# Order of the attention units: the last rows of the first batches as units of their own, behind parts of later batches

## The chip, the cores and the metric

The kernel runs on one core of one Trainium2 chip. Its time is device time in microseconds (us) for one execution: TensorE (PE in the profile), VectorE (DVE), ScalarE (ACT), GpSimd (POOL) and SyncE (SP, which issues DMAs here) work side by side on instruction streams of their own, and the time ends with the last of them. Times of the kernel before are the median of three runs; one further execution was profiled.

## The reference

Two blocks in a row, on 8 batches of 576 rows. The first is attention with 8 heads of 64 columns, in which each row keeps its 32 largest scores; the second is a two-layer MLP on the rows that result.

```python
scores = scale * np.matmul(q, k.transpose(0, 1, 3, 2))      # (8, 8, 576, 576)
kth = np.partition(scores, -32, axis=-1)[..., -32:-31]
attn = softmax(np.where(scores >= kth, scores, -1e9))
x = np.matmul(attn, v).transpose(0, 2, 1, 3).reshape(8, 576, 512)
xn = (x - mean(x)) / np.sqrt(var(x) + 1e-6) * g_ln          # per row
out = x + np.maximum(xn @ w_ch1, 0.0) @ w_ch2               # 512 -> 2048 -> 512
```

q, k and v come as float32; the MLP's gain and weights come as float64, which the kernel reads as pairs of 32-bit words and turns into float32 itself.

## The kernel before, in words

**Units.** A unit is 128 query rows of two heads (a head pair, hp 0 to 3): two tiles of 128 x 576 scores. 576 rows are four such row tiles (qt 0 to 3) and 64 last rows (qt = `J` = 4), which for the two heads share one tile of 128 partitions: a *rest* unit, half as much work for VectorE. There are 8 x 4 x 5 = 160 units. A *job* is one head pair of one batch with a list of row tiles; its units form one group, whose weights are turned into one `pt` tile and multiplied with v together. The list `jobs` (L1027 to L1034) sets the order: for every batch a few *parts* (lists of row tiles), and in each part the four head pairs. Before, batch 0 has the parts [0, 1], [2, 3], [4]; batch 1 has [0, 1], [2, 3, 4]; all later ones [0, 1, 4], [2, 3].

**The step loop** (L1212 to L1361). Step n runs a stage of several units, so that every engine has work: scores of unit n + 2 (TensorE, then ScalarE copies them to `sc`), the selection of unit n on VectorE, the mask of unit n - 1 (ScalarE L496, GpSimd L499) and its exponentials (ScalarE L507), the turning of unit n - 2's weights, and values, output transposes and normalisation of a group that ended two to four units ago. VectorE's selection (`halve`, `select`) first takes the maximum and the minimum of a row's two halves (`hi`, `lo`, L425 and L426), then four rounds of the 8 largest and their replacement (L447, L433); it has two `hi` buffers. GpSimd's `watched` (L466) reads `hi` at the end, so the halving of unit u + 2 waits for the `watched` of unit u.

**Turning.** The weights of a unit must be transposed for the values matmul. Where `u.moved` is set (L1058), VectorE transposes in blocks of 32 (L538) and five DMAs through DRAM do the rest (`move`: one out, four back into `pt`); otherwise TensorE transposes them (L565) and ScalarE copies from PSUM. Before, from the fifth job on, every unit but the last of its group and the rests is moved: 88.

**Heads.** q and k of a head pair are loaded (`load`, L294) and turned by VectorE (`turn_heads`, L326, three transposes) at the pair's first job. The turned k and the later part of q are also written to DRAM (`keep_heads`, pool `turned_kq`, two buffers per head pair, L85), and a later job of the same batch and pair fetches them back (`fetch_heads`). Each job also loads its v (`load_values`) and copies v's last rows into the single tile `ends` (`fill_ends`, GpSimd).

**The MLP.** 256 rows make a block: the row tiles of a part, or the rests of four batches (two head-pair-complete row tiles). A block is *given* (`give`) some steps after the last head pair of its rows is through; then its 64 hidden matmuls (L779) and 56 (the first block: 32 of twice the width, L818) output matmuls (L936) stand in the list `todo`. Eight calls of `fill` in each step take from it as much as `slot(n)` allows: for every later give, the work that will have been given by then, less a reserve of 4 us, is divided by the steps until then, and the least such pace counts. In the first 22 steps it is the difference of the planner's own costs for VectorE and TensorE. After the last unit what is left is worked off without attention between.

**Weights.** 32 pieces of the MLP's weights are loaded, four ahead of the loop and one or two in most of steps 0 to 20 (`batches`). ScalarE and GpSimd split a piece (`split`), VectorE shifts the exponent (`shift`, L176), GpSimd joins it (`join`, L182 and L184). In step n the pieces of `batches[n - 1]` are shifted ahead of the selection (L1236) and joined behind the mask (L1248). When the first block's output is done, GpSimd forms sums of weight blocks (`form_pair`), two of which go to DRAM; later blocks' output matmuls wait for them.

**Start.** L1196 to L1211 load the first two jobs' heads and the first pieces, and compute the scores of units 0 and 1, before the loop; the loads of the second job's q stand on ScalarE's queue.

Of the kernel before, what the change touches and what calls it, by code (L numbers as in the profile page):

```python
# [21 lines left out]
J = 4  # L22
# [7 lines left out]
def compute(  # L30
# [12 lines left out]
    nc = tc.nc  # L43
    P = nc.NUM_PARTITIONS
    B, H, S, D = q.shape
# [5 lines left out]
    NHP = H // 2  # L51
# [5 lines left out]
    def pool(name, bufs, **kw):  # L57
        return ctx.enter_context(tc.tile_pool(name=name, bufs=bufs, **kw))
# [23 lines left out]
    opool = pool("o", 2)  # L82
    xtpool = pool("xt", 1)
    hpool = pool("h", NF // 2)
    turnedpool = pool("turned_kq", 2, space=bass.MemoryType.DRAM)  # L85
    hbmpool = pool("hbm", 4, space=bass.MemoryType.DRAM)
    formpool = pool("forms", 1, space=bass.MemoryType.DRAM)
    psps = pool("ps", 5, space=PSUM)
# [111 lines left out]
    batches = {}  # L200
# [4 lines left out]
    batches = {n: x for n, x in batches.items() if x}  # L205
# [4 lines left out]
    def weights(n, phase):  # L210

        now, coming = batches.get(n, []), batches.get(n + 1, [])
        if phase == 0:
            for x in coming if n < LATE else []:
                x.fetch()
            for x in now[0::2] if n < LATE else []:
                x.split()
        elif phase == 1:  # L220
            for x in now if n >= LATE else now[1::2]:
                x.split()
            for x in coming if n >= LATE else []:
                x.fetch()

    def join_weights(n):
        for x in batches.get(n - 1, []):
            x.join()
# [65 lines left out]
    def load(job, first, second, later=False):  # L294

        job.ins = {}
        for name, src, queue in (("k", k, first), ("q", q, second)):
            t = ldpool.tile([P, S], FP32, tag=name + "in", name=name + "in")

            def part(i, t=t, src=src, queue=queue):  # L300
                head, d0 = 2 * job.hp + i * 32 // D, i * 32 % D
                queue.dma_start(
                    t[i * 32 : (i + 1) * 32, :].rearrange("b (n a) -> b n a", a=32),
                    src[job.b, head, :, d0 : d0 + 32].rearrange("(n b) a -> b n a", b=32),
                )

            for i in range(P // 32):
                if later:
                    age = (4 * len(job.ins) + i) // 2
                    loads.add(lambda i=i, part=part: part(i), -age)  # L310
                else:
                    part(i)
            job.ins[name] = t
# [62 lines left out]
    def scores(u):  # L376

        u.made = [score_half(u, s) for s in range(2)]
        return u.made[0][0][:, HALF:]

    def take_scores(u):
        u.sc = scpool.tile([P, 2, S], FP32, tag="sc", name="sc")
        for t in range(len(u.tiles)):
            for s in range(2):
                nc.scalar.copy(  # L385
                    u.sc[:, t, s * HALF : (s + 1) * HALF], u.made[s][t][:, 0:HALF]
                )
# [25 lines left out]
    def halve(u):  # L413

        nt = len(u.tiles)  # L420
        u.lo = lopool.tile([P, 2, HALF], FP32, tag="lo", name="lo")
        u.hi = hipool.tile([P, 2, HALF + 8 * low_rounds], FP32, tag="hi", name="hi")
        a, b = u.sc[:, 0:nt, 0:HALF], u.sc[:, 0:nt, HALF:S]
        lo, hi = u.lo[:, 0:nt], u.hi[:, 0:nt, 0:HALF]
        nc.vector.tensor_tensor(hi, a, b, ALU.max)  # L425
        nc.vector.tensor_tensor(lo, a, b, ALU.min)  # L426
# [66 lines left out]
    def mask(u, t):  # L493
        if u.e is None:
            u.e = epool.tile([P, 2, S], FP32, tag="e", name="e")
        nc.scalar.activation(  # L496
            u.e[:, t], u.sc[:, t], AF.Relu, bias=u.edge[:, t : t + 1], scale=-STEEP
        )
        nc.gpsimd.tensor_tensor(u.e[:, t], u.e[:, t], u.sc[:, t], ALU.subtract)  # L499
# [56 lines left out]
    def turn(u):  # L556

        g = u.group
        i0 = place_of(u)
        q0 = i0 * 32  # L560

        def part(t):
            ps = turned()
            for c in range(J):
                nc.tensor.transpose(  # L565
                    ps[:, c * P : (c + 1) * P], u.e[:, t, c * P + t * R : (c + 1) * P + t * R],
                    ident[:],
                )
            if u.rest:
                both = ps[:].rearrange("p (c h n) -> p h c n", h=2, n=R)  # L570
                for h in range(2):
                    nc.scalar.copy(
                        g.blocks[:, h, i0 : i0 + R // 32],
                        both[:, h].rearrange("p c (i n) -> p i c n", n=32),
                    )
            else:
                nc.scalar.copy(
                    g.blocks[:, t, i0 : i0 + P // 32],
                    ps[:].rearrange("p (c i n) -> p i c n", c=J, n=32),
                )  # L580

        def last():
            turn_ends(u)()

        heads = () if u.moved else range(len(u.tiles))
        return [lambda t=t: part(t) for t in heads] + [last]
# [58 lines left out]
    def take_values(g):  # L645
        g.oT = otpool.tile([P, GQ], FP32, tag="oT", name="oT")
        nc.scalar.copy(g.oT[:, 0 : g.nq], g.av[:, 0 : g.nq])
# [376 lines left out]

    jobs = []  # L1027
    for b in range(B):
        parts = [[0, 1], [2, 3], [J]]
        if b:  # L1030
            parts = [[0, 1], [2, 3]]
            parts[b < 2].append(J)
        for qts in parts:
            jobs += [Job(b, hp, [qts]) for hp in range(NHP)]  # L1034
    units = []
    for j in jobs:
        j.groups = [Group(j, qts) for qts in j.groups]
# [8 lines left out]
    fresh = []  # L1046
# [8 lines left out]
    CONVERTING = max(n for n in batches if batches[n]) + 2  # L1055
    EARLY = jobs[NHP].first

    for u in units[EARLY:]:  # L1058
        u.moved = not u.rest and u is not u.group.units[-1]


    for j, after_j in zip(jobs, jobs[1:] + [None]):
# [14 lines left out]
    for j in jobs:  # L1077
        if j.hp == NHP - 1:
            b = j.b
# [26 lines left out]
    def at(i):  # L1106
        return units[i] if 0 <= i < N else None
# [92 lines left out]
        x.fetch()  # L1200
    turn_heads(fresh[0])
    nc.sync.dma_start(grow[:], g_ln.rearrange("(c p) -> c p", p=P))
    load(fresh[1], nc.sync, nc.scalar)
    scores(units[0])
    take_scores(units[0])
    halve(units[0])
    scores(units[1])
    take_scores(units[1])
# [3 lines left out]
    for n in range(END):  # L1212
# [8 lines left out]
        u, nxt, mk = at(n), at(n + 1), at(n - 1)  # L1221
# [3 lines left out]
        parts = turn(ex) if ex and not ex.moved else []  # L1225
# [7 lines left out]
        if quick:  # L1233
            values(g)
            take_values(g)
        for x in batches.get(n - 1, []):  # L1236
            x.shift()
        spare = None
        for x in ahead:
# [4 lines left out]
        if mk:  # L1244
            prepare(mk)
            for t in range(len(mk.tiles)):
                mask(mk, t)
        join_weights(n)  # L1248
        if mk and doubt is not None:
            watch(mk)  # L1250
        if plain_done[0] is not None and plain_done[0] < n - 1:
# [85 lines left out]
        if last_rest and last_rest.rest and last_rest.job.b % 2:  # L1337
            hp = last_rest.job.hp
# [9 lines left out]
            select(u, 3)  # L1348
        if nxt:
            halve(nxt)  # L1350
        weights(n, 1)
        if g and not quick and g.job.hp == NHP - 1:
            for qt in g.qts:
# [18 lines left out]
@with_exitstack  # L1372
def kernel(
    ctx: ExitStack,
    tc: tile.TileContext,
    *operands: bass.AP,
):
    nc = tc.nc
    doubt = ctx.enter_context(tc.tile_pool(name="doubt", bufs=1)).tile(
        [1, 1], I32, tag="doubt", name="doubt"  # L1380
    )
    compute(tc, *operands, low_rounds=1, doubt=doubt[:])
    again = nc.values_load(  # L1383
        doubt[:], min_val=0, max_val=1,
        skip_runtime_bounds_check_because="a comparison's result",
    )
    with tc.If(again > 0):
        compute(tc, *operands, low_rounds=2, doubt=None)
# [31 lines left out]
```

## Time and profile before

| | us |
|---|---|
| median of 3 runs | 1628.69 (1627.76 to 1628.86) |
| the profiled execution | 1625.28 |
| its span, first to last instruction | 1623.1 |
| busy: PE / DVE / ACT / POOL | 1486.5 / 1370.2 / 1058.0 / 1030.9 |
| mean granted TensorE clock | 0.965 of full |

The profile page gives for each engine its busy time, its share of the span and its instructions; then the span in 40 slices with one digit each for the busy share in tenths, and the clock granted to TensorE in tenths (PEclk). A table by stretch has one row for each piece of time: its ends and length, the busy time of PE, PEld (TensorE's weight loads), DVE, ACT and POOL with the number of instructions, the granted clock, the DMA engines' mean share and the GB/s they moved. A line of the waits has the waiting instruction, "<-" what released it, and the total, the number and the longest of these waits in us. A line in order of time has start, length, engine, source line and operation, and in brackets the idle time before it. Ends of matmuls are modelled, and the span is some 2 us shorter than the execution's own time.

### The profile page before, as it was taken

What the parts mean: (1) busy time and instruction counts of PE and PEld (TensorE: products, weight loads), DVE (VectorE), ACT (ScalarE), POOL (GpSimd) and SP (SyncE); (2) the same over time, 40 slices, a digit from 0 to 9 for tenths busy, and PEclk for the clock granted to TensorE, in tenths of its full rate; (3) what the DMA queues carried; (4) which work ended last, traced back from release to release, by engine and by line L of the source; (5) the groups of instructions that cost most, each with busy time, mean ns of one, the idle gap of its engine ahead of it and who ended that gap; (6) DMA issues with size and microseconds to landing.
All of it is one profiled execution on the core that took longest, in us unless ns stands there. A gap on an engine that the chain in (4) does not pass through costs nothing. (4 is left out here: it accounts for less than half of the span.)

```text
span 1623.1 us, 27069 instructions
## 1 busy us (share of the span) xinstructions
PE 1486.5 (92%) x7770; PEld 1124.5 (69%) x7770; DVE 1370.2 (84%) x3971; ACT 1058.0 (65%) x2984; POOL 1030.9 (64%) x1489
## 2 busy tenths in 40 slices
PE   3579678689979899999999999999999999999997
PEld 2346346467757677777777777777777777778886
DVE  5997978989999999999999999999999989882000
ACT  5878765566757686777666767677677766763221
POOL 6878976855546565667566747576657574746244
PEclk9779989799989999999999999999999999999999
DMA  6625644444646456445564556546554554522211
GB/s 159 167 69 160 195 119 130 153 138 118 197 121 202 126 144 172 158 152 133 162 192 131 142 148 176 161 122 174 144 174 149 146 148 156 157 90 85 71 34 54
DMA packets 367206, 228.27 MB, mean 141 GB/s; under 512 B 248772, under 2 KB 337352, under 8 KB 367048
## 3 DMA queue, kind: packets, MB, share of 16 engines
q1 hardware_dynamic: 362312, 225.86, 48.5%
q8 instruction: 64, 1.05, 0.3%
q10 hardware_dynamic: 4736, 0.59, 0.2%
q14 instruction: 94, 0.77, 0.2%
HBM read 154.01 MB, written 72.35 MB: 139 GB/s over the span
## 5 line engine op out<-in xcount | busy, mean ns | idle before, releaser
L499 POOL TENSOR_TENSOR e<-e,sc 128x576 f32<-128x576 f32 x288 | 405.1, 1425 | 421.7 <-ACT e L496 323.9
L779 PE MATMUL hps<-xT,w 128*128 128x256 f32 x2304 | 542.1, 385 | 6.0 <-ACT xT L741 3.8
L779 PEld LDWEIGHTS hps<-xT,w 128*128 128x128 f32 x2304 | 430.3, 193 | 76.2 <-issue 10.8
L447 DVE MAX8 m<-hi 128x8 f32<-128x296 f32 (+1 forms) x1152 | 469.8, 442 | 0.1
L433 DVE MATCH_REPLACE8 hi<-m,hi 128x288 f32<-128x288 f32 (+1 forms) x864 | 377.1, 441 | 0.0
L936 PE MATMUL ops<-w,h 128*128 128x256 f32 x1360 | 322.4, 384 | 3.4 <-DMA w<-forms 3.4
L936 PEld LDWEIGHTS ops<-w,h 128*128 128x128 f32 x1360 | 254.0, 193 | 41.7 <-issue 5.0
L496 ACT ACTIVATE e<-sc,m 128x576 f32<-128x576 f32 x288 | 209.3, 769 | 90.1 <-PE scps L599 89.0
L507 ACT ACTIVATE e<-e,m 128x576 f32<-128x576 f32 x288 | 226.8, 790 | 32.3 <-POOL e L499 31.3
L385 ACT COPY sc<-scps 128x288 f32<-128x288 f32 x576 | 187.0, 402 | 63.3 <-POOL e L499 49.8
L425 DVE TENSOR_TENSOR hi<-sc 128x576 f32<-128x576 f32 (+1 forms) x160 | 134.3, 840 | 68.4 <-POOL watched L466 64.0
L802 ACT ACTIVATE h<-hps 128x512 f32<-128x512 f32 x144 | 87.3, 607 | 121.3 <-PE hps L779 120.7
L632 PE MATMUL av<-pt,vb 128*64 128x256 f32 (+2 forms) x1088 | 143.2, 405 | 0.8 <-ACT pt L604 0.6
L426 DVE TENSOR_TENSOR lo<-sc 128x576 f32<-128x576 f32 (+1 forms) x160 | 135.4, 846 | 0.0
L538 DVE STREAM_TRANSPOSE sc<-e 128x512 f32<-128x512 f32 x176 | 113.9, 682 | 22.3 <-ACT e L507 22.3
L404 PE MATMUL scps<-kT,late_qT 64*128 64x288 f32 (+3 forms) x832 | 123.4, 415 | 7.8 <-ACT sc L385 5.7
L936 PE MATMUL ops<-wt,s 128*128 128x256 f32 x544 | 128.7, 381 | 0.4 <-POOL s L866 0.4
L439 DVE MAX8 hi<-lo 128x8 f32<-128x288 f32 x288 | 117.5, 443 | 0.0
L404 PE MATMUL scps<-kT,qT 64*128 64x288 f32 x512 | 91.7, 470 | 24.8 <-DVE qT L331 23.5
L565 PE MATMUL tp<-ident,e 128*128 128x128 f32 x448 | 73.3, 291 | 44.6 <-ACT e L507 29.7
L936 PEld LDWEIGHTS ops<-wt,s 128*128 128x128 f32 x544 | 100.1, 190 | 16.0 <-issue 2.3
L404 PEld LDWEIGHTS scps<-kT,late_qT 64*128 64x128 f32 (+1 forms) x832 | 70.6, 169 | 58.0 <-issue 18.0
(107 smaller groups left out, 1846.5 us busy)
## 6 DMA issues: line engine op xcount, KB each, us to landing
turned<-sc SPq DMA_DIRECT2D x88, 512.0 KB, 2.9
pt<-turned SPq DMA_DIRECT2D x352, 128.0 KB, 2.8
w<-forms SPq DMA_DIRECT2D x136, 256.0 KB, 4.1
vb<-in_v_dram SPq DMA_DIRECT2D x68, 288.0 KB, 3.6
raw<-in_moe_w_ch_dram SPq DMA_DIRECT2D x32, 512.0 KB, 5.3
kT<-kept SPq DMA_DIRECT2D x36, 288.0 KB, 3.3
kin<-in_k_dram SPq DMA_DIRECT2D x128, 72.0 KB, 2.6
kept<-kT SPq DMA_DIRECT2D x32, 288.0 KB, 3.0
```

The lines of the kernel that those rows point to most:

```text
L385: nc.scalar.copy(u.sc[:, t, s * HALF : (s + 1) * HALF], u.made[s][t][:, 0:HALF])
L404: nc.tensor.matmul(ps[i * R : i * R + ql, o : o + width], qT[r, q0 : q0 + ql], kT[r, k0 : k0 + width], start=True, stop=True,)
L425: nc.vector.tensor_tensor(hi, a, b, ALU.max)
L426: nc.vector.tensor_tensor(lo, a, b, ALU.min)
L433: nc.vector.match_replace(x, m[:, t, :], x, LOWEST)
L447: nc.vector.max(m[:, t, :], u.hi[:, t, 0:width])
L496: nc.scalar.activation(u.e[:, t], u.sc[:, t], AF.Relu, bias=u.edge[:, t : t + 1], scale=-STEEP)
L499: nc.gpsimd.tensor_tensor(u.e[:, t], u.e[:, t], u.sc[:, t], ALU.subtract)
L507: nc.scalar.activation(u.e[:, t], u.e[:, t], AF.Exp, bias=u.bias[:, t : t + 1], scale=-scale, accum_out=g.den[:, col : col + 1],)
L632: nc.tensor.matmul(av[h * D : (h + 1) * D, 0 : g.nq], vb[:, h * (J + 1) + c, :], g.blocks[:, h, 0 : g.nq // 32, c, :], start=(c == 0), sto ...
L779: nc.tensor.matmul(ps[0][:, side * N : (side + 1) * N], w1[:, c, f * P : (f + 1) * P], self.xT[:, c, 0:N], start=(c == 0), stop=(c == NC - 1),
L936: nc.tensor.matmul(bank[name][:, 0:Q], a(j), rhs, start=first and j == 0, stop=(j == G - 1), skip_group_check=not first,)
```

## The change

`jobs` is no longer built by a loop over batches. A list `order` of (batch, row tiles) is written out: batch 0's rows 0 to 3, then batch 1's, then half of batch 2, and only then the rests of batch 0 as four jobs of one unit each; the rests of batches 1, 2 and 3 follow in the same way behind parts of later batches. Batches 4 and 5 have their rests with rows 2 and 3. Batches 6 and 7 have them with rows 0 and 1, and their rows 2 and 3 come last of all. That makes 80 jobs in place of 68, and lone rests in steps 40 to 43, 60 to 63, 72 to 75 and 84 to 87, where before the only four stood in steps 16 to 19. As the heads of up to three batches are now needed again later, `turned_kq` gets five buffers.

`moved` is set job by job: a unit is moved unless it is a rest or the last of its job; in batches from 2 on the last unit of head pairs 0 and 2 is moved too, unless a rest follows. 92 units are moved.

At the start the loads of the second job stand behind the first unit's scores and their copies. The four pieces of `batches[-1]` are shifted at the end of step 0, behind the halving of unit 1, and joined after that; from step 1 on both stand where they stood.

```diff
-    turnedpool = pool("turned_kq", 2, space=bass.MemoryType.DRAM)
+    turnedpool = pool("turned_kq", 5, space=bass.MemoryType.DRAM)
...
-    jobs = []
-    for b in range(B):
-        parts = [[0, 1], [2, 3], [J]]
-        if b:
-            parts = [[0, 1], [2, 3]]
-            parts[b < 2].append(J)
-        for qts in parts:
-            jobs += [Job(b, hp, [qts]) for hp in range(NHP)]
+    rows, rest = ([0, 1], [2, 3]), [J]
+    order = [(0, rows[0]), (0, rows[1]), (1, rows[0]), (1, rows[1])]
+    order += [(2, rows[0]), (0, rest), (2, rows[1]), (3, rows[0]), (1, rest)]
+    order += [(3, rows[1]), (2, rest), (4, rows[0]), (3, rest), (4, rows[1] + rest)]
+    order += [(5, rows[0]), (5, rows[1] + rest)]
+    order += [(6, rows[0] + rest), (7, rows[0] + rest), (6, rows[1]), (7, rows[1])]
+    assert B == 8
+    jobs = [Job(b, hp, [qts]) for b, qts in order for hp in range(NHP)]
...
-    for u in units[EARLY:]:
-        u.moved = not u.rest and u is not u.group.units[-1]
+    for j, nj in zip(jobs, jobs[1:] + [None]):
+        for u in units[max(j.first, EARLY) : j.last + 1]:
+            u.moved = not u.rest and (
+                u.i < j.last or (j.b > 1 and j.hp % 2 == 0) and nj is not None and not units[nj.first].rest
+            )
...
-    load(fresh[1], nc.sync, nc.scalar)
     scores(units[0])
     take_scores(units[0])
+    load(fresh[1], nc.sync, nc.scalar)
     halve(units[0])
...
-        for x in batches.get(n - 1, []):
+        for x in batches.get(n - 1, []) if n else []:
             x.shift()
...
-        join_weights(n)
+        if n:
+            join_weights(n)
...
         if nxt:
             halve(nxt)
+        if n == 0:
+            for x in batches[-1]:
+                x.shift()
+            join_weights(0)
         weights(n, 1)
```

## The prediction

> **What bounds the kernel now.** I read the page's busy shares and slices first, then the same numbers by stretches of the planner's steps, then the waits of VectorE (DVE), then single steps in order of time. Step n begins where VectorE starts the n-th `hi<-sc` maximum (L425, counted from 0); everything below is cut there.
>
> The page, busy shares and slices of 40.6 us:
>
> ```profile
> PE 1486.5 (92%) x7770; PEld 1124.5 (69%) x7770; DVE 1370.2 (84%) x3971; ACT 1058.0 (65%) x2984; POOL 1030.9 (64%) x1489
> ...
> PE   3579678689979899999999999999999999999997
> ...
> DVE  5997978989999999999999999999999989882000
> ...
> PEclk9779989799989999999999999999999999999999
> ```
>
> TensorE (PE) has holes in the first fourteen slices, VectorE stops three slices before the end, and TensorE alone runs on. The same by stretch; the cuts are the starts of steps 20, 32, 88 and 149:
>
> ```profile
> core 0: us, PE busy (x) PEld busy (x) DVE busy (x) ACT busy (x) POOL busy (x), PEclk, DMA share, GB/s
> 0.00:227.50 227.50, 149.30 (x699) 93.19 (x699) 187.57 (x513) 171.90 (x436) 179.95 (x193) 0.89 0.55 151
> 227.50:352.00 124.50, 101.68 (x513) 73.22 (x513) 109.00 (x300) 70.84 (x205) 85.09 (x112) 0.88 0.44 128
> 352.00:825.20 473.20, 449.95 (x2404) 339.07 (x2403) 462.71 (x1371) 331.55 (x975) 289.11 (x439) 0.97 0.54 154
> 825.20:1365.40 540.20, 538.89 (x2918) 415.62 (x2917) 511.30 (x1494) 377.61 (x1091) 348.60 (x529) 1.00 0.53 153
> 1365.40:1623.10 257.70, 246.64 (x1242) 203.44 (x1240) 99.59 (x295) 106.07 (x281) 128.20 (x220) 0.99 0.28 87
> ```
>
> Call them A to E. In C VectorE works 462.71 of 473.20 us: it sets the pace. In D it idles 28.9 us and TensorE is full; in E TensorE alone counts. What ends VectorE's idle time in steps 10 to 31 (113.7 to 352 us):
>
> ```profile
> DVE hi L425 <- POOL watched L466: 17.8, 10, 3.9
> DVE wt L176 <- POOL wt L164: 14.6, 9, 3.5
> ```
>
> There GpSimd (POOL), busy with the weight conversion, is the last to release VectorE. So three regimes: GpSimd with VectorE in A and B, VectorE in C, TensorE in D and E. Steps 50, 51 and 52 in order of time show VectorE's price of a unit:
>
> ```profile
> 501.57 0.73 DVE L425 TENSOR_TENSOR hi<-sc 128x576 f32<-128x576 f32 x1
> 509.12 0.70 DVE L425 TENSOR_TENSOR hi<-sc 128x288 f32<-128x288 f32 x1
> 513.43 1.30 DVE L538 STREAM_TRANSPOSE sc<-e 128x512 f32<-128x512 f32 x2
> 514.99 0.74 DVE L425 TENSOR_TENSOR hi<-sc 128x576 f32<-128x576 f32 x1
> ```
>
> A bare whole unit takes 7.55 us (501.57 to 509.12). A last-row unit ("rest") takes some 4.2: step 51 is 5.87, with a move of 1.37 (1.30 busy and its start-up) and a little waiting.
>
> **What the skill says.** The Trainium skill, "Perfetto Trace Analysis", Identifying the Most-Contended Engine, warns that matmul busy time is no measure of how full TensorE is. The trace agrees: C shows it 95% busy while the steps have VectorE's length, so I add up matmuls instead. "TensorE: Matmul & The Clock Gate", Part 1, says that the array falls to half its clock after about 3.4 us idle; here the granted clock is 0.89, 0.88 and 0.97 in A, B and C against 1.00 in D, so holes there cost twice. "SBUF — State Buffer", Who interferes with whom, says that a VectorE instruction with two SBUF inputs contends with a GpSimd instruction that reads SBUF: the halving pair of step 1 took 1.37 and 1.82 us under GpSimd's joins, and 0.76 and 0.75 in step 0 without them.
>
> **The change, part by part.** One MLP matmul is two records; 78 records in 17.00 us at 1454.78 (L779) make 0.436 us each. The order of both programs gives the MLP matmuls per stretch, before and after: B 117 and 130, C 641 and 690, D 823 and 745, E 465 and 481. A has 90 in both. The planner spreads what has been given until the next batch rows arrive. With rows 0 to 3 of batches 0 and 1 coming without rests between them, rows arrive at steps 9, 20, 28, 36 and not at 9, 19, 32, 44, and the pace is some 12.5 a step from step 22 to 148, steps 26 to 28 apart, where the formed weights are awaited (before: 9 to 10, then 12, then 14). About 78 matmuls, 34 us, leave D, where they are on the path, for B and C, where TensorE had holes. That is the gain; the rest is cost.
>
> *A.* Steps 0 to 15 process the same units. Without the four shifts behind the first halving VectorE loses waits of 2.67, 3.12 and 1.20 us in step 0, and with ScalarE's four load issues (2.99 us at 7.12) behind the first score copies it starts about 2 us sooner. But the four joins on GpSimd (11.2 us, 22.07 to 33.3) now start only after the second halving, and step 2's halving waits for GpSimd's `watched` behind them; before, that row ended 0.1 to 2.1 us ahead of the halving in steps 2 to 9. So of the 9 us I take 1; the bounds are +2 and -7. Steps 16 to 19 hold whole units where four rests stood. Those rests took 41.5 us; whole units under conversion took 10.90, 12.44 and 10.64 (steps 13 to 15), 45.2 for four: +3.7. Two more head turns (1.41 us each) half hidden: +1.6. A: 227.5 - 1 + 3.7 + 1.6 = 232.
>
> *B.* Twelve whole units and no rest. Steps 20 and 21 like before, 22. Steps 23 to 26 are GpSimd's: subtract 2.8, form pair 5.2 to 6.4, 1.6 hidden banks of 1.36, small ones 0.5, or 11.2 each, 45. The other six at some 10 (before: 9.3 to 11.5, and 13.8 after a burst of 11.8 us of MLP that is now 9.2): 61. B: 128, against 124.5.
>
> *C.* Forty whole units and sixteen rests (before 43 and 13). VectorE in the whole ones: 40 x 7.55 = 302, 27 moves x 1.37 = 37, 8 head turns x 1.4 = 11, 2 pairs of row statistics x 1.6 = 3, 353; VectorE-bound steps ran 1 to 2% over such sums (steps 52 to 59: 69.6 for 68.8), so 359. The rests now stand in four runs of four. A run costs VectorE 20 us but TensorE 35: 50 MLP matmuls 21.8, and scores (1.2 a unit), transposes (0.6 a bank), values (2.65 for 256 columns, 1.12 for 64) and output transposes (0.38) less their overlap, 13.5. How far may TensorE fall behind? Its lateness reaches VectorE through ScalarE's in-order queue, the subtraction and `watched`: when TensorE is ahead, `watched` ends 4.2 us after the selection (steps 37 to 44), in D 6 to 9, and then the halving waits. So a run absorbs 3 to 5 us, which the whole units behind it give back. A run: 32; four: 128. C: 487, against 473.2.
>
> *D.* Forty-five whole units, sixteen rests, interleaved as before: 340 + 66, 41 moves 56, 12 head turns 17, 6 pairs of statistics 10, 489 of VectorE, and TensorE with 745 x 0.436 = 325 and 150 of attention at 475, no longer over it. Before, 823 x 0.436 + 160 = 519 ran in 540. In steps 56 to 76, TensorE at 0.94 of VectorE, the time was 178.7 for a VectorE sum of 173, 1.033. I take 1.04: 507, against 540.2, or -33.
>
> *E.* 16 more MLP matmuls and two row turns, +7.9; steps 149 to 155 have matmuls enough where they had not, -2.5. E: 263.
>
> The twelve more lone rests bring twelve more head fetches (two DMAs each) and twelve value loads, and four more moves bring five DMAs each, on SyncE's queue. At some 0.75 MB a rest beside a DMA share of 0.53 I cost them nothing; the step of margin between fetch and scores hides them, and without it each would cost its 3.3 us landing time. The larger DRAM pool costs nothing.
>
> Sum of the span: 232 + 128 + 487 + 507 + 263 = 1617, against 1623.1: about -6. The rows are of an execution of 1625.28 us; the three runs' median is 1628.69. I put the median at 1622.
>
> **The rivals.** *Runs of rests stall (slower).* Each lone rest refills the one `ends` tile: TensorE's values, GpSimd's refill, TensorE's next values. The only lone rests of before took 41.5 us, with a wait of 3.42 us on `ends` at 228.42. For it: the same buffers. Against: there the refill stood behind weight joins. If a run costs 37 and not 32, +20: 1642. It decides from a run of 34.5 on. *VectorE and GpSimd keep D slow.* D's idle ends on `watched`, which also follows GpSimd's own queue; at 1.07 of VectorE's sum D takes 522 and the whole 1637, slower too. *Only re-dealt.* A and B come 6 us dearer than I say, since nothing there is TensorE's: 1628, the same. *More absorbed.* Runs at 28 and D at 497: 1622 - 16 - 10 = 1596; TensorE's waits of the first slices speak for it.
>
> **How the numbers follow.** Forecast (1605 to 1625) 0.45; more absorbed 0.12; only re-dealt 0.14; stalling runs 0.20; slow D 0.09. 0.2% of 1628.69 is 3.3 us, about what a measurement of this kernel can tell from no change. Faster 0.57, same 0.14, slower 0.29. The range leaves a tenth on each side: 1603 to 1643. The forecast's own is 1605 to 1625.
>
> **What would show it.** Step 88 of the new program should start near 847 us, later than before's 825.2; step 149 near 1354, earlier than 1365.4; VectorE's idle time between them under 20 us, not 28.9; and each run of four 128x288 halvings should span 30 to 34 us. TensorE's holes in slices 6 to 14 should shrink. I am wrong if the runs span over 35 us, if D does not come under 515, or if step 32 starts past 368.

## The result, and the profile after

| us | before | after |
|---|---|---|
| median | 1627.76 (8 runs, 1626.18 to 1628.95) | 1618.16 (8 runs, 1612.28 to 1624.14) |
| ratio after to before | | 0.9941 (95%: 0.9922 to 0.996) |
| the profiled execution / its span | 1625.28 / 1623.1 | 1617.02 / 1615.1 |

The kernel is faster by 0.6%, some 10 us. After's runs lie further apart (0.7%) than before's (0.2%), so differences between profiles of a few microseconds are read with care below.

First the page of the kernel after, its busy shares and its slices (40.4 us each):

```profile
PE 1487.4 (92%) x7954; PEld 1131.2 (70%) x7954; DVE 1371.2 (85%) x3979; ACT 1057.7 (65%) x2988; POOL 1033.9 (64%) x1513
...
PE   3578769799999999999999999999999999999997
...
DVE  5997998899989997999978999999999999666100
```

The busy times of TensorE's matmuls and of the other three engines moved by 3 us at most (TensorE's weight loads grew by 7), so nothing was saved in work. What changed is where TensorE's holes are: before, slices 6 to 14 read `786899798`, now `697999999`. The holes that C had (from slice 9 on) are filled. VectorE works on a little longer at the end (the 666 before the last 100).

The table by stretch of the kernel after, cut as before at the starts of steps 20, 32, 88 and 149 (ends, length, busy PE, PEld, DVE, ACT, POOL with counts, clock, DMA share, GB/s):

```profile
0.00:233.30 233.30, 152.79 (x656) 95.83 (x657) 201.51 (x562) 176.26 (x442) 186.39 (x196) 0.86 0.55 150
233.30:356.70 123.40, 107.84 (x525) 77.67 (x526) 114.10 (x323) 77.27 (x217) 89.21 (x113) 0.87 0.47 133
356.70:837.00 480.30, 472.61 (x2784) 367.09 (x2783) 448.79 (x1319) 339.86 (x993) 302.66 (x477) 1.00 0.61 171
837.00:1349.50 512.50, 505.60 (x2748) 384.85 (x2746) 498.45 (x1472) 357.36 (x1058) 320.32 (x505) 1.00 0.57 162
1349.50:1615.10 265.60, 248.58 (x1247) 205.73 (x1246) 108.34 (x309) 106.98 (x279) 135.28 (x223) 0.99 0.30 94
```

| | A | B | C | D | E | span |
|---|---|---|---|---|---|---|
| before | 227.5 | 124.5 | 473.2 | 540.2 | 257.7 | 1623.1 |
| forecast | 232 | 128 | 487 | 507 | 263 | 1617 |
| after | 233.3 | 123.4 | 480.3 | 512.5 | 265.6 | 1615.1 |
| after less before | +5.8 | -1.1 | +7.1 | -27.7 | +7.9 | -8.0 |

One stretch gains and three pay for it. D lost 27.7 us. MLP matmuls counted in the two traces between VectorE's marks are 822.5 in D before and 756.5 after, 66 or 28.8 us fewer; 49 of these are now in C, 10 in E and 6.5 in B. (In the order of the program 78 leave D. TensorE runs behind VectorE's marks, so some of what belongs to C is worked off in D.) In D after, TensorE is still busy in 505.6 of 512.5 us, and VectorE now in 498.5. VectorE's idle time in D is 14.0 us (before 28.9). What ends VectorE's waits in steps 10 to 31 (113.7 to 356.7 us) after:

```profile
DVE hi L425 <- POOL watched L466: 13.3, 8, 3.9
DVE wt L176 <- POOL wt L164: 7.3, 5, 2.0
```

Both are GpSimd's and both are smaller than before (17.8 and 14.6). Inside C, the four runs of lone rests (28.8, 30.5, 30.0 and 29.6 us) and the whole units between them, from the table by stretch:

```profile
356.70:429.60 72.90, 72.22 (x403) 55.38 (x402) 72.83 (x221) 53.29 (x153) 48.53 (x74) 1.00 0.70 196
429.60:458.40 28.80, 28.80 (x185) 22.37 (x184) 20.86 (x61) 20.75 (x63) 9.97 (x16) 1.00 0.57 173
458.40:605.20 146.80, 141.96 (x799) 109.17 (x798) 146.33 (x430) 101.47 (x291) 98.46 (x156) 0.99 0.60 167
605.20:635.70 30.50, 29.50 (x189) 23.14 (x188) 21.96 (x61) 21.65 (x65) 10.85 (x16) 1.00 0.56 167
635.70:705.60 69.90, 69.90 (x421) 55.28 (x419) 69.03 (x211) 51.17 (x152) 51.12 (x81) 1.00 0.49 145
705.60:735.60 30.00, 29.34 (x187) 22.48 (x186) 25.10 (x68) 20.50 (x62) 18.26 (x29) 1.00 0.64 174
735.60:807.40 71.80, 71.29 (x427) 56.51 (x426) 71.02 (x213) 51.63 (x148) 47.08 (x75) 1.00 0.68 183
807.40:837.00 29.60, 29.60 (x189) 22.77 (x189) 21.66 (x61) 19.39 (x61) 18.39 (x33) 1.00 0.57 168
```

The DVE column carries the whole units: 72.83 of 72.90, 146.33 of 146.80, 69.03 of 69.90, 71.02 of 71.80. The PE column carries the runs: TensorE is busy 117.2 of their 118.9 us, VectorE 89.6. But TensorE is nearly full in the whole units too, so this table does not say by itself which engine sets them. Two experiments do.

### The profile page after: what moved, and what is told of

Same layout as the page of the kernel before. It is cut to its first block, busy times and chain, and to the rows that moved or that the text cites. A ratio compares the mean times of both kernels' runs of the same rounds, so it can differ in the third digit from the quotient of the medians.

```text
span 1615.1 us, 27577 instructions
## 1 busy us (share of the span) xinstructions
PE 1487.4 (92%) x7954; PEld 1131.2 (70%) x7954; DVE 1371.2 (85%) x3979; ACT 1057.7 (65%) x2988; POOL 1033.9 (64%) x1513
## 4 chain that ended last, share of the span: by engine, by line
PE 51%; DVE 25%; POOL 10%; DMA 5%; ACT 5%; issue 2%; SPq 1%; ACTq 0%; DVEq 0%; POOLq 0%
PE hps L779 20%; PE ops L936 15%; DVE m L447 7%; DVE hi L433 6%; PE scps L404 6%; PE av L632 5%; POOL e L499 4%; DVE sc L538 3%; DVE lo L426 2%; DVE hi L425 2%; DVE hi L439 2%; DMA pt<-turned 2%; DMA turned<-sc 2%; PE av L639 2%; PE tp L565 2%
## 5 line engine op out<-in xcount | busy, mean ns | idle before, releaser
L496 ACT ACTIVATE e<-sc,m 128x576 f32<-128x576 f32 x288 | 209.3, 769 | 70.4 <-PE scps L599 69.6
L632 PE MATMUL av<-pt,vb 128*64 128x256 f32 (+2 forms) x1280 | 148.9, 375 | 5.5 <-DMA kept<-kT 2.4
L538 DVE STREAM_TRANSPOSE sc<-e 128x512 f32<-128x512 f32 x184 | 119.2, 684 | 12.5 <-ACT e L507 7.1
L632 PEld LDWEIGHTS av<-pt,vb 128*64 128x64 f32 x1280 | 81.2, 141 | 56.0 <-issue 7.1
## 6 DMA issues: line engine op xcount, KB each, us to landing
pt<-turned SPq DMA_DIRECT2D x368, 128.0 KB, 2.8
```

The source lines that it names most:

```text
L496: nc.scalar.activation(u.e[:, t], u.sc[:, t], AF.Relu, bias=u.edge[:, t : t + 1], scale=-STEEP)
L538: nc.vector.transpose(blocks.rearrange("p (j t c n) -> p j t c n", j=ni, t=2, c=J)[:, :, t], u.e[:, t, t * R : t * R + JP].rearrange("p (c ...
L632: nc.tensor.matmul(av[h * D : (h + 1) * D, 0 : g.nq], vb[:, h * (J + 1) + c, :], g.blocks[:, h, 0 : g.nq // 32, c, :], start=(c == 0), sto ...
```

## The experiments

"Whole" and "runs" below are the two kinds of row of the last table, summed: in the kernel after, whole 361.4 and runs 118.9 us. Ratios are to the kernel before, run beside each.

### Which engine sets the whole units and the runs: tensor_plus and vector_plus

Both add work to steps 32 to 87 (C) of the changed kernel alone, without changing its values.

```diff
 tensor_plus
+                if c == 0 and side == 0 and 31 < now[0] < 88:
+                    nc.tensor.matmul(
+                        ps[0][:, 0:N], w1[:, c, f * P : (f + 1) * P], self.xT[:, c, 0:N],
+                        start=True, stop=True,
+                    )
                 nc.tensor.matmul(
 vector_plus
         nc.vector.tensor_tensor(lo, a, b, ALU.min)
+        if 32 < u.i < 89 and nt == 2 and u.i % 4 != 3:
+            nc.vector.tensor_tensor(lo, a, b, ALU.min)
```

> The changed kernel with 47 hidden matmuls of the MLP done twice in steps 32 to 87 (stretch C), 47 x 0.436 = 20.5 us of TensorE; the second writes the same values over the first. Theory: since the change TensorE sets C's length (busy 472.6 of 480.3 us), so C grows by 15 to 21 us and the kernel takes 1631 to 1640. Rival, the prediction's own view that VectorE sets C and TensorE's work fills holes: C grows by under 8 us, 1618 to 1625.

> The changed kernel with the minimum of the halving done twice for 30 whole units of steps 33 to 87 (stretch C), 30 x 0.75 = 22.5 us of VectorE; the second writes the same values. Theory: TensorE sets C, and VectorE's 31 us of idle time there take most of it: C grows by 0 to 9 us, 1618 to 1627. Rival, the prediction's view that VectorE sets C: it grows by 15 to 23 us, 1632 to 1641.

Measured: tensor_plus 1630.12 us (ratio 1.0021, 1.0008 to 1.0034), vector_plus 1649.19 us (1.014, 1.0122 to 1.0158): 12 and 31 us above the changed kernel. The theory that I held by then gave 15 to 21 us to the TensorE work in C and 0 to 9 to the VectorE work; C grew by 14.1 and 35.4. The rival, the prediction's view, gave under 8 and 15 to 23, so neither held as it was put. The first four rows of C, tensor_plus:

```profile
356.90:430.90 74.00, 74.00 (x408) 57.34 (x408) 73.93 (x222) 52.91 (x153) 48.48 (x74) 1.00 0.69 190
430.90:462.10 31.20, 30.75 (x198) 23.96 (x195) 21.06 (x62) 20.74 (x63) 10.05 (x16) 1.00 0.56 166
462.10:609.80 147.70, 145.11 (x822) 112.84 (x823) 145.97 (x431) 102.16 (x293) 99.22 (x156) 1.00 0.59 165
609.80:641.40 31.60, 31.36 (x201) 24.69 (x198) 21.97 (x62) 21.69 (x65) 10.94 (x16) 1.00 0.55 164
```

and the first two runs of whole units of vector_plus:

```profile
352.50:431.10 78.60, 74.11 (x411) 56.80 (x410) 78.36 (x226) 53.90 (x154) 48.39 (x74) 1.00 0.66 183
...
459.60:622.50 162.90, 147.06 (x810) 112.37 (x809) 162.42 (x442) 101.15 (x291) 102.21 (x156) 0.97 0.54 150
```

Lengths in C, whole and runs, of all kernels that keep the changed order of C:

| | whole | runs | C |
|---|---|---|---|
| after | 361.4 | 118.9 | 480.3 |
| tensor_plus | 366.4 (+5.0) | 128.0 (+9.1) | 494.4 |
| vector_plus | 396.8 (+35.4) | 118.9 (0.0) | 515.7 |
| order_76 | 349.0 (-12.4) | 130.7 (+11.8) | 479.7 |
| weighted | 357.4 (-4.0) | 106.9 (-12.0) | 464.3 |
| pace_held | 364.2 (+2.8) | 123.6 (+4.7) | 487.8 |

VectorE's extra work (its busy time in C rose from 448.79 to 484.45, by 35.7) comes out whole, 35.4 us, in the whole units. The edit left the rests alone, so it says nothing of VectorE's worth in the runs. TensorE's 20.5 us come out at 14.1. In the order of the program 17 of the 47 added matmuls (7.4 us) stand in the steps of the runs and 30 (13.1 us) in those of the whole units; the runs grew by 9.1 us and the whole units by 5.0, so TensorE carries part of its work from the whole units into the runs behind them. In the whole units VectorE is idle for only 2.2 of 361.4 us. So VectorE sets the whole units, with TensorE close behind it, and TensorE sets the runs, as the prediction had it. What fell is my theory that TensorE had become the limit of all of C, read off a PE column that was 98% full, and with it the rival's view that TensorE's work would mostly fill holes.

### The rule of what is moved: order_76, and the same in the old order, before_76

```diff
 order_76 (on the changed kernel)
-    for j, nj in zip(jobs, jobs[1:] + [None]):
-        for u in units[max(j.first, EARLY) : j.last + 1]:
-            u.moved = not u.rest and (
-                u.i < j.last or (j.b > 1 and j.hp % 2 == 0) and nj is not None and not units[nj.first].rest
-            )
+    for u in units[EARLY:]:
+        u.moved = not u.rest and u is not u.group.units[-1]
 before_76 (on the kernel before)
         u.moved = not u.rest and u is not u.group.units[-1]
+        if u.job.b in (1, 2, 3) and len(u.group.units) == 3 and u.i == u.job.first + 1:
+            u.moved = False
```

> The changed kernel with the old rule for moved units: every unit but the last of its job and the rests, which makes 76 and not 92. Sixteen moves fewer take 16 x 1.37 = 22 us from VectorE (ten of them between steps 32 and 87, two up to step 148, four after) and give TensorE some 16 x 1.2 = 19 us and ScalarE as much. My theory, VectorE sets the pace to step 87 and TensorE after step 149: 10 x 1.37 less a little in the first, +5 in the last, 1610 to 1620, near the changed kernel's 1618. Rival, the turned units are where the gain comes from: TensorE's 19 us come back, 1630 to 1637.

> The kernel before with 12 fewer units moved, 76 in all: in the groups of three of batches 1 to 3 only the first unit is moved, which lies in steps 20 to 80. Theory: a move costs VectorE 1.37 us and TensorE's turning fills holes that C has anyway, so C gets 8 to 14 us shorter, in the old order too: 1613 to 1620, and half or more of what order_76 has over the kernel before is not from the order. Rival: TensorE and ScalarE pay as much for the turning as VectorE saves: 1624 to 1632.

Measured: order_76 1610.24 us (0.9899, 0.988 to 0.9919), 8 us faster than the change as it was made; before_76 1623.69 us (0.9984, 0.9975 to 0.9993), a gain of 3. C and D of order_76, and the wait of its VectorE in C:

```profile
356.40:836.10 479.70, 479.03 (x2866) 373.08 (x2865) 437.83 (x1299) 351.79 (x1014) 307.64 (x477) 1.00 0.54 150
836.10:1344.60 508.50, 505.69 (x2770) 385.62 (x2768) 494.79 (x1466) 361.01 (x1064) 321.57 (x505) 1.00 0.55 157
```

```profile
DVE hi L425 <- POOL watched L466: 33.4, 16, 4.1
```

In C, ten fewer moves take 11 us off VectorE. The whole units get 12.4 us shorter, and the runs 11.8 us longer: TensorE, which now turns those units itself, arrives later at the runs (22 more MLP matmuls, 9.6 us, fall between their marks, though the program has as many of them in those steps), and VectorE waits for `watched` 33.4 us instead of 23.1. Nothing is left of it. In D, three fewer moves and 3.7 us less of VectorE come out at 4.0 us. The profiles differ by 5.4 us of span, D being most of it; the rest of the 8 is within the spread of runs. The time lies in the range of the theory, but not on its grounds: C was to get shorter by about ten moves, E longer by 5 us, and neither did. before_76 shows the same balance in the old order: VectorE's busy time in C fell by 9.9 us (462.71 to 452.84), its wait on `watched` there rose from 8.2 to 17.3, and C went from 473.2 to 472.0, where the theory asked for 8 to 14 us. So the 16 extra moves cost 8 us where the whole change gained 10, and the order, at 76 moves and with the new start, which the next experiment finds to be worth nothing, is worth 1623.69 - 1610.24 = 13 us (the two were run in different sets, whose kernels before had medians 0.2 us apart).

### The start alone: start_alone

The kernel before with the edits of the start and nothing else.

```diff
-    load(fresh[1], nc.sync, nc.scalar)
     scores(units[0])
     take_scores(units[0])
+    load(fresh[1], nc.sync, nc.scalar)
...
-        for x in batches.get(n - 1, []):
+        for x in batches.get(n - 1, []) if n else []:
...
-        join_weights(n)
+        if n:
+            join_weights(n)
...
+        if n == 0:
+            for x in batches[-1]:
+                x.shift()
+            join_weights(0)
```

> The kernel before, with only the start of the change: loads of the second job behind the first score copies, the first four shifts and joins at the end of step 0. My theory: step 0 loses its waits of 7 us and the first halving comes 1 to 2 us sooner, but GpSimd's four joins start later by as much, and the halving of step 2 waits for GpSimd; by step 10 no more than 1 us is left. 1626 to 1628.5, ratio 0.999 to 1.0005. Rival, the early gain is kept because VectorE sets the pace afterwards: 1619 to 1621, ratio 0.995, and the order of units would then be worth nothing.

Measured: 1625.92 us, ratio 0.9994 (0.9983 to 1.0004): no difference. Where the time goes is seen in VectorE's waits from 0 to step 10 of this kernel:

```profile
DVE hi L425 <- POOL watched L466: 9.1, 2, 8.7
```

Before, the same line stood at 0.4 us. In the changed kernel step 1 begins at 19.5 us instead of 29.1, but step 2 at 40.1 instead of 42.0 and step 10 at 113.1 instead of 113.7, with the same wait (8.4, the longest 8.1).

### Where the MLP stands: pace_held and weighted

pace_held keeps the early rows from being spent early; weighted halves the pace in the sixteen steps of lone rests and raises it elsewhere.

```diff
 pace_held
+        if 31 < n < 56:
+            even = min(even, 4.4)
         return max(0.0, even) / SLOTS
 weighted
+    def room(n):
+        u = at(n)
+        return 0.5 if u and u.rest and len(u.group.units) == 1 else 1.0
...
-                    even = min(even, (left - RESERVE) / (m - n))
+                    even = min(even, (left - RESERVE) * room(n) / sum(map(room, range(n, m))))
```

> The changed kernel with the MLP's pace held at 4.4 us a step in steps 32 to 55, as it was in the kernel before; 39 MLP matmuls (17 us) go from steps 32 to 87 into steps 88 to 148 (651 and 784 of them in place of 690 and 745). My theory, the gain is work taken out of the late stretch: steps 44 to 59 keep their time because VectorE sets it, the run of rests at step 40 gets 4 us shorter, and steps 88 to 148 get 8 to 14 us longer, 1622 to 1628. Rival, the pace does not matter and the order itself gains by other waits: 1612 to 1616.

> The changed kernel with the planner's pace halved in the sixteen steps of a lone rest, 26 MLP matmuls in a run of four in place of 49; the others go mostly to steps 88 to 148 (799 in place of 745). My theory, a run is as long as TensorE's work in it: a run falls from about 30 us to 21 to 24, four of them 24 to 36 us in all, and steps 88 to 148 get 12 to 20 us longer because TensorE's sum (499) passes VectorE's (489) there: 1598 to 1612. Rival, a run is held by the one tile of v's last rows, which TensorE and GpSimd hand to each other: runs stay at 29 to 30 us and the late steps get longer, 1630 to 1638.

Measured: pace_held 1637.46 us (1.006, 1.004 to 1.008); weighted 1615.54 us (0.9939, 0.9915 to 0.9962). C and D of pace_held:

```profile
361.00:848.80 487.80, 466.17 (x2707) 358.06 (x2706) 447.77 (x1320) 338.81 (x989) 292.39 (x458) 0.98 0.60 167
848.80:1374.40 525.60, 521.08 (x2814) 399.57 (x2815) 503.48 (x1472) 363.22 (x1063) 336.02 (x524) 1.00 0.56 160
```

and of weighted:

```profile
354.90:819.20 464.30, 451.73 (x2692) 349.57 (x2691) 449.18 (x1319) 336.23 (x988) 293.55 (x459) 1.00 0.63 176
819.20:1343.10 523.90, 521.95 (x2827) 401.08 (x2827) 501.46 (x1471) 361.50 (x1063) 334.25 (x524) 1.00 0.56 160
```

pace_held returns half of the MLP matmuls that the order had taken from D (784 in D in place of 745, 39 x 0.436 = 17.0 us), and D grows by 13.1, as expected (8 to 14). The kernel lost 19 us in the median and not the 4 to 10 expected. Its profiled execution, 1643.72 us, is the longest of its five and 26.8 us of span over the changed kernel's. Of these A and B have 4.3, where the edit changes nothing, C 7.5, though it has 39 fewer MLP matmuls, and E 1.9. In C the third and fourth row of whole units, which now take more MLP work, are 3.4 and 2.9 us longer, with TensorE busy in 73.3 of 73.3 and 74.2 of 74.7 us. And the first run of rests, which was to be 4 us shorter, is 3.3 longer (32.1 us). With 38 MLP matmuls there instead of 48, TensorE comes to the values of a unit before the transfers in front of them have landed:

```profile
442.97 3.68 PE L632 MATMUL av<-pt,vb 128*64 128x256 f32 x16 [5.09 <-DMA late_qT<-kept]
454.74 1.95 PE L632 MATMUL av<-pt,vb 128*64 128x256 f32 x16
```

It stands still for 5.1 us. The record of the granted clock shows half of full speed from 441.5 to 448.3 us, beginning 3.6 us after TensorE fell idle, and the same 16 matmuls take 3.68 us there and 1.95 in the next group: this hole cost twice, as the prediction says of holes. VectorE then waits 7.8 us for `watched`; the longest such wait in the changed kernel's C is 3.7. So the MLP matmuls in this run also cover transfers, which neither the prediction nor this experiment's expectation had counted. Of the 20.6 us that C and D lose here, D's 13.1 are what half of its relief is worth; the rest has these other causes.

weighted gave its runs 26 or 27 MLP matmuls instead of 48 to 50, in the order of the program. They shrank by 12 us to 26.7 each, not to the 21 to 24 that I expected for VectorE's 20. With the prediction's own terms TensorE needs 26 x 0.436 + 13.5 = 24.8 in a run, and it is busy 24.8; VectorE is busy 23.2. What holds the remaining 2 us was not tested. C got 16.0 us shorter, D 11.4 longer, and the medians differ by 2.6 us, less than their spread; the profiled execution is the fastest of its five. At 1615.54 the kernel lies outside the 1598 to 1612 of the theory and far below the rival's 1630.

### Both edits: weighted_76

The diff of order_76 and that of weighted, together.

> The changed kernel with two edits at once: the old moved rule (76 moved, as in order_76) and the MLP pace halved in the sixteen lone-rest steps (as in weighted). Theory: the two edits act on different things (order_76 takes VectorE work out of stretch C, weighted takes TensorE work out of the runs of rests), so what each was worth against the changed kernel adds up: 1618 - 8 - 3 = 1607, range 1602 to 1611. Rival: with less VectorE work the whole steps of C are TensorE's, and work pushed out of the runs into them costs its full price: 1612 to 1620, slower than order_76's 1610.

Measured: 1612.1 us, ratio 0.9911 (0.9894 to 0.9927); order_76 had 0.9899 (0.988 to 0.9919). The gains do not add: C 461.7 and D 525.4 give 987.1, order_76's 479.7 and 508.5 give 988.2. The time is the rival's, but not its place: in C, where it expected work pushed out of the runs to cost its full price, weighted_76 is 18.0 us shorter than order_76. D, which has 54 more MLP matmuls (23.5 us), is 16.9 us longer, and weighted's D grew by 11.4 for as many. A likely reason is that TensorE had 2.8 us of idle time in order_76's D and 6.9 in the changed kernel's.

### Lone rests one by one: single_76

order_76 with each lone rest directly behind a head pair of the part that it follows, instead of four in a row.

```diff
-    jobs = [Job(b, hp, [qts]) for b, qts in order for hp in range(NHP)]
+    jobs = []
+    for (b, qts), (nb, nqts) in zip(order, order[1:] + [(0, [])]):
+        if qts == rest:
+            continue
+        for hp in range(NHP):
+            jobs.append(Job(b, hp, [qts]))
+            if nqts == rest:
+                jobs.append(Job(nb, hp, [rest]))
```

> order_76 with the lone rests set one by one behind the head pairs of the part they follow, instead of four in a row; 76 moved, 695 MLP matmuls in C and 768 in D. Theory: a run of four rests costs some 32 us, 12 more than VectorE needs for it, and whole units beside it take only part of this back, so that interleaved rests, as D has them, save a part of 4 x 12 us: 1592 to 1605. Rival: TensorE's total in C is the limit, however it is spread (it was busy 472.6 of 480.3 us in the changed kernel's C): 1607 to 1614, as order_76.

Measured: 1620.78 us, ratio 0.9956 (0.994 to 0.9972): 10 us slower than order_76, worse than both theories said. C is 484.3 and D 513.5, 4.6 and 5.0 us longer. TensorE's longest wait in C of single_76,

```profile
PE av L632 <- DMA pt<-turned: 4.4, 2, 2.5
```

has no counterpart in order_76: values wait for the transfers of a moved unit. A likely reason is that the step between is short where it holds a rest; no run tests that, nor how much of C's 4.6 us these 4.4 are. The 5.0 us of D are not settled, with as many MLP matmuls in both. In any case the clustering of rests was not a cost that spreading them in this way saves.

### Where the rests stand: attached, first_attached and end_76

attached has no lone rests: batches 0 to 5 have them with rows 2 and 3. first_attached does so for batch 0 alone. end_76 takes batches 6 and 7 in plain order. All three have the old moved rule (with the fewer groups of attached it moves 92 units, with those of first_attached 80).

```diff
 attached
-    order = [(0, rows[0]), (0, rows[1]), (1, rows[0]), (1, rows[1])]
-    order += [(2, rows[0]), (0, rest), (2, rows[1]), (3, rows[0]), (1, rest)]
-    order += [(3, rows[1]), (2, rest), (4, rows[0]), (3, rest), (4, rows[1] + rest)]
-    order += [(5, rows[0]), (5, rows[1] + rest)]
+    order = []
+    for b in range(6):
+        order += [(b, rows[0]), (b, rows[1] + rest)]
     order += [(6, rows[0] + rest), (7, rows[0] + rest), (6, rows[1]), (7, rows[1])]
 first_attached
-    order = [(0, rows[0]), (0, rows[1]), (1, rows[0]), (1, rows[1])]
-    order += [(2, rows[0]), (0, rest), (2, rows[1]), (3, rows[0]), (1, rest)]
+    order = [(0, rows[0]), (0, rows[1] + rest), (1, rows[0]), (1, rows[1])]
+    order += [(2, rows[0]), (2, rows[1]), (3, rows[0]), (1, rest)]
 end_76
-    order += [(6, rows[0] + rest), (7, rows[0] + rest), (6, rows[1]), (7, rows[1])]
+    order += [(6, rows[0] + rest), (6, rows[1]), (7, rows[0] + rest), (7, rows[1])]
```

> The changed kernel without any lone rest: batches 0 to 5 have their rests with rows 2 and 3, batches 6 and 7 as changed; old moved rule, 92 moved; first rows are given at steps 9, 24, 32, 44 as before rather than 9, 20, 28, 36; 687 MLP matmuls in C, 802 in D. Theory: it is the early coming of the rows that pays, since it moves MLP matmuls out of D; here D has 42 more of them than order_76, 18 us: 1618 to 1628. Rival: what paid was taking the four lone rests out of the conversion steps 16 to 19 and the re-ordered end, and lone rests later only cost: 1603 to 1612.

> order_76 with only the rests of batch 0 set differently: with its rows 2 and 3, as in the kernel named attached, so that lone rests are those of batches 1 to 3; 80 moved; first rows given at 9, 24, 32, 40 rather than 9, 20, 28, 36. A and B should be 18 to 23 us shorter (attached: 333.5 for both, order_76: 356.4), with 31 fewer MLP matmuls in B (13.5 us), which come back in C and D. Theory: what counts is TensorE's idle time before step 32, and that was the same in both (99.5 us in attached, 97.4 in order_76): 1605 to 1613. Rival: most of the shorter start is kept, because attached lost it only at its end (E 272.7 against 265.1): 1590 to 1602.

> order_76 with batches 6 and 7 in plain order: rows 0 and 1 with the rests of batch 6, its rows 2 and 3, then batch 7 likewise. 712 MLP matmuls in C, 775 in D, 466 in E, where order_76 has 703, 760 and 491. Theory: the end's new order only moves matmuls between stretches that TensorE sets anyway: C and D together some 10 us longer, E some 11 us shorter, the kernel 1606 to 1614, as order_76. Rival: the new end is a good part of the gain, since in the plain order the last rows come late and TensorE waits for them: 1617 to 1625.

Measured: attached 1617.46 us (0.9942, 0.9925 to 0.9958), first_attached 1606.98 us (0.9871, 0.9855 to 0.9888), end_76 1610.11 us (0.9898, 0.988 to 0.9915). The first four stretches of first_attached:

```profile
0.00:224.00 224.00, 143.09 (x598) 87.05 (x598) 191.69 (x514) 166.06 (x415) 181.13 (x191) 0.88 0.56 148
224.00:336.90 112.90, 93.93 (x458) 65.07 (x458) 110.99 (x318) 74.11 (x211) 82.85 (x102) 0.86 0.56 160
336.90:826.60 489.70, 487.55 (x2854) 378.28 (x2853) 456.23 (x1360) 360.57 (x1033) 307.59 (x478) 1.00 0.54 148
826.60:1340.00 513.40, 511.90 (x2800) 391.42 (x2799) 497.31 (x1466) 362.87 (x1066) 327.20 (x514) 1.00 0.55 157
```

A and B are 19.5 us shorter than order_76's 356.4, and C and D give 14.9 of it back (28 MLP matmuls come to them from B, 12.2 us). What remains, 3 us in the medians, is in the expected range, but the two intervals overlap; by its median this version is the fastest of all that were run. attached lies between its two expectations and is as fast as the change itself, on other grounds: A 222.5 and B 111.0, but D 528.2 and E 272.7. Lone rests set late are not needed for a gain of this size; first_attached, which has attached's first steps and the change's later order, is faster than either, but it moves 80 units where both move 92, and order_76 has shown what such moves cost. end_76 is worth the same as order_76: D is 6.4 us longer and E 10.3 shorter. The new order of the end is worth nothing that can be measured. (The stretch counts of MLP matmuls in the expectations of single_76, attached, first_attached and end_76 are too high for some stretches: in the order of the program order_76 has 690, 745 and 481 in C, D and E, as the changed kernel.)

## Why the prediction was right, point by point

The median was put at 1622.0 and is 1618.16, and the mechanism, MLP work taken out of a full D, is what the table by stretch shows. That the sum of the span came within 2 us (1617 for 1615.1) is in part luck: the stretches are off by +1.3, -4.6, -6.7, +5.5 and +2.6, which nearly cancel, and the whole gain is 8.

**A, 232: 233.3.** The start was to keep 1 of 9 us: step 10 came 0.6 us earlier, and the start alone changes the kernel by nothing that can be measured. The joins on GpSimd take it back at step 2, as the step said. Whole units in place of rests in steps 16 to 19: 46.1 us for 41.5, +4.5 (said: +3.7). Steps 10 to 15 with the head turns: +1.9 (said: +1.6, though two turns of 1.41 half hidden are 1.4).

**B, 128: 123.4.** Steps 20 and 21 took 18.3 us, not 22, and steps 23 to 26 42.2, not 45; the other six took 62.9, not 61. Steps 20 and 21 were set "like before", though the kernel before turned a head in step 21 and waited for GpSimd (4.1 us in the two), and the new one does neither.

**C, 487: 480.3.** The whole units, at 359 by VectorE's sum, took 361.4. (Two readings behind these numbers are a little off: steps 52 to 59 of the kernel before took 69.3 us, not 69.6, and VectorE is busy 22.4 us in a run, where 20 had been set.) The runs, at 32 each, took 29.7, two of them under the 30 to 34 that was named as the sign. Three runs together show the mechanism of this step: VectorE's added time comes out whole in the whole units (vector_plus), TensorE's in the runs first (tensor_plus), and taking MLP work from the runs shortens them (weighted). The mis-sized term is what a run absorbs: 35 less 3 to 5 had been forecast; TensorE's 35 less 29.7 is 5.3. The trace has the same amount: of the 48 to 50 MLP matmuls of a run's steps only 37.6 fall between VectorE's marks, and the 11 or 12 others, 5 us, are carried into the whole units behind. These gave back less than 3 us of it (361.4 for 359).

**D, 507: 512.5.** In the order of the program the matmuls that left D were right, 78; but the prediction sends all of them to B and C, and by its own counts 16 of them (7 us) go to E, where TensorE sets the time (its sum for E does price them). How far D lives on them pace_held shows. The mis-sized term is what was put on VectorE's sum: 507 is 1.037 times 489 (1.04 would have been 508.6), and 512.5 / 489 = 1.048 came; order_76, with three moves fewer (485), has 508.5 / 485 = 1.048 too. Of the 23.5 us over the sum 14.0 are VectorE's idle time (said: under 20); the other 9.5 are VectorE's busy time, 498.5, so the price of its work was too low as well (16 rests at 4.2 are 67 and not 66, the least of it). D now lies close to the balance of the two engines: 3.7 us less of VectorE gave 4.0 us (order_76), and 17.0 us more of TensorE cost 13.1 (pace_held), 54 matmuls or 23.5 us more cost 11.4 (weighted).

**E, 263: 265.6.** It is 7.9 us longer, the whole first term of the forecast; the 2.5 us that were to be saved did not come. TensorE waits 6.7 us in E, where it waited 1.2 before. That the end's order only shifts time between D and E was not in the prediction; end_76 shows it.

**The rivals.** *Runs of rests stall* fell: they span 28.8 to 30.5 us, none near 34.5, and no wait for `ends` of more than 0.4 us is among TensorE's there. *VectorE and GpSimd keep D slow* asked for 522, and D has 512.5. *Only re-dealt* asked for A and B 6 us dearer; they came 3.3 cheaper. *More absorbed* is where C went part of the way, 29.7 against its 28, but D did not follow.

**What the prediction did not see.** It priced the moved units in VectorE's sums and never asked what the kernel would be without the 16 that the new rule adds. Without them it is 8 us faster. The twelve more head fetches and value loads were costed at nothing, and order_76, which has all of them, shows no wait of TensorE on a transfer in C. The changed kernel has 4.1 us of such waits there (2.4 and 1.7), and without the extra moves they are gone.

## What to carry to other kernels

Where two engines are both nearly full, a busy column does not tell which of them sets the time; adding a known amount to each, in that stretch alone, did so here, and showed that one sets some steps and the other the rest. Work moved from one of the two engines to the other can come back in the steps that the other sets, as it did in order_76, so look at each kind of step and not at the stretch's sum. The gain of an order that brings work early was here what the later, full stretch lost; the next engine's sum in that stretch bounds it, here VectorE's 489 us with 5% on top. Work taken out of a place may also have covered a transfer there, as pace_held shows, so look for what would then be waited for.

## What the hardware showed that was not expected

The second minimum of vector_plus, the same instruction on the same data, can cost more than twice the first. In order of time:

```profile
509.11 0.74 DVE L426 TENSOR_TENSOR lo<-sc 128x576 f32<-128x576 f32 x1
509.65 3.35 POOL L501 TENSOR_TENSOR e<-e,sc 128x576 f32<-128x576 f32 x2 [3.84 <-ACT e L498]
509.89 1.84 DVE L428 TENSOR_TENSOR lo<-sc 128x576 f32<-128x576 f32 x1
```

The first runs before GpSimd's mask multiplication starts and takes 0.74 us; the second runs beside it and takes 1.84. Over the 30 of them the mean is 1.35 us (0.76 to 1.86), so the 22.5 us meant to be added were 40 (VectorE's busy time in C rose by 35.7, since its other instructions took some 5 us less in sum). The Trainium skill, "SBUF — State Buffer", Who interferes with whom, says that a VectorE instruction with two SBUF inputs contends with a GpSimd instruction that reads SBUF, and this trace agrees: the one that starts 0.8 us later, beside GpSimd, takes 1.10 us longer.

The other is the spread: the changed kernel's eight runs lie between 1612.28 and 1624.14 us with mean granted clocks from 0.953 to 0.971. The two fastest have the highest clock, but the slowest, at 0.963, is not the one with the lowest; no run here says why.
